# The last pair's second layer as three passes over 12-bit words, in a state-space and ELU layer kernel on one core

## Chip, cores and metric

The kernel runs on one core of a Trainium2 chip. The metric is device time in microseconds (us) of one execution, as the median of several runs. TensorE (PE) multiplies, VectorE (DVE), ScalarE (ACT) and GpSimd (POOL) work element by element, SyncE (SP) issues most transfers. All data that the engines touch lies in SBUF, products arrive in PSUM (eight banks; GpSimd can't reach them).

## What is computed

A chunked state-space scan (4 batches, 8 heads, 768 steps, head width 32, state 16) gives x, a matrix of 3072 tokens by 256. Two dense layers with an ELU between them follow. Cut to the part that matters here:

```python
def _moe_ref(x, w_in, w_out):          # x 3072x256, w_in 256x2048, w_out 2048x256
    h = x @ w_in
    g = np.where(h > 0.0, h, np.exp(np.minimum(h, 0.0)) - 1.0)
    return (g @ w_out).astype(np.float32)
```

All of it is float32.

## The kernel before

**Blocks, pairs and stages.** Tokens are taken in 12 blocks of 256 (`NP` = 12) and, from block 2 on, in pairs (2, 3), (4, 5) up to (10, 11). The inner dimension of 2048 is cut into `MC` = 16 slices m of 128. Every engine runs its instructions in the order in which the code issues them; tiles come from pools in which a tag has a fixed number of buffers that go round, so that a new tile waits for the last use of the tile whose buffer it takes. The loop `for n in range(4, NP, 2)` (L1310) is a row of stages. In the stage of n the pair (n, n+1) goes through the first layer, one slice m = k per step (`l1_words`, L778), while the generator `second(n - 2)` (L871) puts the second layer of the pair before between these products, three or four steps at a time (`l2s`). The stage of n = 10 is the last: it has no scan work left (`m` is None). Behind the loop the second layer of the last pair, `second(10, True)`, runs alone (L1355).

**First layer in words.** An f32 product takes TensorE several passes. The first layer instead cuts both operands into a high word and a rest of about 12 bits, held as f32 tiles of type F32R, which one pass multiplies. Scaled words are used so that three passes give the product: `high` collects w1·y1 and w0·y0, `both` collects the product of the two mixed words, and `WORD - 1` and `WORD` (2 to the 12th) bring the scales together (L788 to L800). ELU follows: L805 and L806 on ScalarE, L813 on VectorE, which writes `g_of[n, m]`, a tile of 128 x 2 blocks x 256 tokens. `end_words` runs one step late (`late`).

**Second layer by sums.** `second` uses seven products in the place of eight (a Strassen-Winograd scheme) on quarters of g and of `w_out`, in plain f32. Sums of activations are made by GpSimd through `sub` (L848): one for every even slice in `end_words` (L816), `sum_t2` (L863), and the eight per half behind products 0 and 1 (L920 to L927). They are made in place, in `g_of`. Of the weights, `a_out` holds four quarters of `w_out`, of which `a_out[2]` (named s1 or a21) was overwritten in place by its sum with `a_out[3]` (`plus`, L1280), and `s_out` holds three more sums, in tiles of tag "w64". Each half of the inner dimension runs seven products r of four steps, whose results VectorE adds into `c`. In the last call (`last`) the second half stores its parts as they are done, with one product split into two (L888 to L900).

**Pools that the change uses.** "w64" (11 buffers: raw weights, then weight sums and the words of w_in), "w_in" (9: the weights and then their third words w0), "g0" and "g1" (12 each: g_of), "L", "bct", "ctm", "xr", "bc", "M", "ec", "b" (scan tiles, out of use in the last stage), "yT" (2), "t2" (4). Of PSUM `p_a` has 7 banks and `p_o` one.

Of the kernel before, what the change touches and what calls it, by code (L numbers as in the profile page):

```python
# [10 lines left out]
F32 = mybir.dt.float32  # L11
U32 = mybir.dt.uint32
BF16 = mybir.dt.bfloat16
F32R = mybir.dt.float32r
ALU = mybir.AluOpType
ACT = mybir.ActivationFunctionType

P = 128
Q = 64
BLK = 2 * P  # L20
CW = 256
WORD = 2.0 ** 12
NEAR = 1.0 + 2.0 ** -13
# [9 lines left out]
def kernel(  # L33
# [27 lines left out]
    nc = tc.nc  # L61
# [3 lines left out]
    NP = NB * NG  # L65
    BH = NB * NH
    ROWS = BH * NG
    DM, DF = moe_w_in.shape
    w_in64, w_out64 = moe_w_in.bitcast(U32), moe_w_out.bitcast(U32)
    KC, MC = DM // P, DF // P  # L70
# [12 lines left out]
    def psum(shape, name):  # L83
        return p_a.tile(shape, F32, tag="a", name=name)
# [7 lines left out]
    for k in range(4):  # L92
        (nc.scalar if k % 2 else nc.sync).dma_start(
            out=la0[BH * k:BH * (k + 1)],
# [715 lines left out]
    def end_words():  # L810
        n, m, h, e = late.pop(0)
        g_of[n, m] = ffn.tile([P, 2, BLK], F32, tag=f"g{m % 2}", name="g", bufs=12)
        nc.vector.scalar_tensor_tensor(  # L813
            out=g_of[n, m].rearrange("p b i -> p (b i)"), in0=e, scalar=1.0, in1=h,
            op0=ALU.subtract, op1=ALU.max)
        if m % 2 == 0 and (n, m) != (2, 14):  # L816
            sub(g_of[n, m][:, 1], g_of[n, m][:, 1], g_of[n, m][:, 0])

    def row_of(n):
        b, g = place(n)  # L820
        return b * S + g * BLK
# [25 lines left out]
    def sub(out, in0, in1):  # L847
        nc.gpsimd.tensor_tensor(out=out, in0=in0, in1=in1, op=ALU.subtract)  # L848

    def quarters(n, i):  # L850


        if n == 2 and i < DIRECT:
            A, B = g_of[n, i], g_of[n + 1, i]
            return A[:, 0], A[:, 1], B[:, 0], B[:, 1]
        A, B = g_of[n, 2 * i], g_of[n, 2 * i + 1]
        return A[:, 0], B[:, 0], A[:, 1], B[:, 1]
# [10 lines left out]

    c_of = {}

    def second(n, last=False):  # L871


        c = c_of[n] = ffn.tile([P, 2, 2, 2, P], F32, tag="c", name="c_sum", bufs=1)
        c11, c12, c21, c22 = (c[:, at, :, e] for e in range(2) for at in range(2))
        a11, a12, s1, a22 = a_out
        s2, s3, s4 = s_out
        for half in range(2):
            if not half:
                tmp = ffn.tile([P, 3, 2, P], F32, tag="tmp", name="p_sum", bufs=1)  # L880
                p1, p5, u = (tmp[:, r] for r in range(3))
            chunk = range(4 * half, 4 * half + 4)

            def add(out, in0, in1, eng=nc.vector):
                eng.tensor_tensor(out=out, in0=in0, in1=in1, op=ALU.add)

            for r, a in enumerate((a11, a12, s1, s2, s3, a22, s4)):
                if last and half and r == 6:  # L888
                    store(n, 0)
                    for ts, queue in enumerate((nc.scalar, nc.sync)):  # L890
                        ps = psum([P, P], "ps_o")
                        for i in chunk:
                            nc.tensor.matmul(  # L893
                                out=ps, lhsT=quarters(n, i)[3][:, ts * P:(ts + 1) * P],
                                rhs=a[:, i], start=(i == chunk[0]), stop=(i == chunk[-1]))
                        nc.vector.tensor_tensor(
                            out=c12[:, ts], in0=ps, in1=c12[:, ts], op=ALU.add)
                        r0 = row_of(n + 1) + ts * P
                        queue.dma_start(out=out[r0:r0 + P, 0:P], in_=c12[:, ts])
                    return  # L900
                pool, tag = (p_a, "a") if (7 * half + r) % 2 else (p_o, "o")
                ps = pool.tile([P, 2, P], F32, tag=tag, name="ps_o")
                for i in chunk:
                    b11, b21, b12, b22 = quarters(n, i)
                    b = (b11, b21, b12, t2_of[n, i], b11, b21, b22)[r]
                    for ts in range(2):
                        nc.tensor.matmul(  # L907
                            out=ps[:, ts], lhsT=b[:, ts * P:(ts + 1) * P], rhs=a[:, i],
                            start=(i == chunk[0] and ts == 0), stop=(i == chunk[-1]),
                            skip_group_check=True)  # L910
                    if i < chunk[-1]:
                        yield
                if r == 0:
                    if half:
                        add(p5, ps, c22)
                        add(c21, ps, c21)
                        add(c11, ps, c11)
                    else:
                        nc.scalar.copy(out=p1, in_=ps)
                    for i in chunk:  # L920
                        b11 = quarters(n, i)[0]
                        sub(b11, t2_of[n, i], b11)
                elif r == 1:
                    add(c11, ps, c11 if half else p1)
                    for i in chunk:
                        b21 = quarters(n, i)[1]
                        sub(b21, b21, t2_of[n, i])  # L927
                elif r == 2:
                    add(p5, ps, p5 if half else p1)
                elif r == 3:  # L930
                    add(p5, ps, p5)
                    if half:
                        add(c12, c12, p5, nc.gpsimd)
                        add(c21, ps, c21)
                    else:
                        add(u, ps, p1)
                elif r == 4:
                    if half:
                        add(c21, ps, c21)
                    else:  # L940
                        add(u, ps, u)
                    add(c22, ps, p5)
                    if not half:
                        nc.scalar.copy(out=c12, in_=ps)  # L944
                    if last and half:
                        r0 = row_of(n + 1)
                        nc.sync.dma_start(
                            out=out[r0:r0 + BLK, P:2 * P].rearrange("(t p) c -> p t c", p=P),
                            in_=c22)
                    if not half:  # L950
                        sum_t2(n, 1)
                    elif n + 2 < NP:
                        sum_t2(n + 2, 0)
                elif r == 5:
                    add(c21, ps, c21 if half else u)
                elif half:
                    add(c12, ps, c12)
                else:
                    nc.vector.tensor_tensor(out=c12, in0=ps, in1=c12, op=ALU.subtract)
                yield  # L960

    def store(n, at):
        r0 = row_of(n + at)
        nc.sync.dma_start(
            out=out[r0:r0 + BLK, :].rearrange("(t p) e -> p t e", p=P),
            in_=c_of[n][:, at].rearrange("p t e c -> p t (e c)"))
# [343 lines left out]
    for n in range(4, NP, 2):  # L1310
        m = n + 2 if n + 2 < NP else None
        steps = second(n - 2)

        def l2s(count):
            for _ in range(count):
                next(steps)

        for k in range(16):
            l1_words(n, k, between=m if k == 15 else None)
            turn_step(n, k // 2 * 2 + 1, k % 2)  # L1320
            if n == 4 and k == 0:
                decay(6, 1)
            if m:
                stage_scan(n, k)
            begin_end()
            if k == 0 and n > 4:
                store(n - 4, 0)
                store(n - 4, 1)
            if not m:
                l2s(4 if k % 2 else 3)  # L1330
                continue
            l2s((3 + (n == 4), 3 - (n == 4), 3, 3, 3, 3, 3, 3, 4 + 4 * (n == 4), 5 - 4 * (n == 4),
                 2, 2, 3, 1, 1, 0)[k])
            if k == 9:
                scores(m, m + 1)
                sums(m, m + 1)
                for q in range(4):
                    weigh_two(m, q)
                l2s(2)
                states(m)  # L1340
            if k == 10:
                states(m + 1)
            if k == 13:
                y = across(m, m + 1)
                inside(y, m, m + 1, ts=(0,))
                l2s(4)
                inside(y, m, m + 1, ts=(1,))
        if m:
            l2s(4)
            both_of_y(m)  # L1350
        end_words()
        for _ in steps:
            pass
    n = NP - 2
    for k, _ in enumerate(second(n, True)):  # L1355
        if k == 0:
            store(n - 2, 0)
            store(n - 2, 1)


# [28 lines left out]
```

## Time and profile before

| what | value |
|---|---|
| runs before | 347.66, 347.88, 347.88 us, median 347.88 |
| the profiled execution, its own time | 347.65 us |
| its span in the profile | 345.9 us |
| granted TensorE clock over the span | 0.999 |
| TensorE idle in all, by its busy time | 345.9 - 338.7 = 7.2 us |
| longest wait of TensorE | 1.1 us (the first product) |
| L799 and L813, VectorE, 72 each | 0.69 us each, one operand in PSUM |
| L848, GpSimd, 128x256 | 0.73 us each (the "g<-t,g" group: 721 to 740 ns) |

The page of the profile gives busy time by engine, the span in 40 slices, the chain of work that ended last, and groups of instructions by line. PE is the matmul side of TensorE, PEld its weight loads, which overlap it. A timeline line is: start, duration, engine, line, operation, output<-inputs, shapes, count; where a count is over 1 the duration is that of the whole run. An f32 product shows as two records. A group is one line of the code with one set of operands; where a helper such as `sub` issues everything, its line stands for many places, and the tile names tell them apart.

### The profile page before, as it was taken

The numbers are of one execution on the slowest core, as the hardware profiler recorded it, in microseconds if no ns is written. First come the engines' busy times: TensorE is split into PE (matmuls) and PEld (weight loads), VectorE is DVE, ScalarE is ACT, GpSimd is POOL, SyncE is SP. The second block draws the span as 40 slices with busy tenths as digits, with TensorE's granted clock in tenths as the row PEclk, the third lists the DMA queues.
The fourth block names the chain that finished last, engine by engine and source line by source line (L and its number), as shares of the span: only waits on it lengthen the run. The fifth ranks groups of instructions, "written<-read, shape, count | busy, mean of one in ns | idle before, by whom it ended". The sixth has DMA issues, their size and how long they took to land.

```text
span 345.9 us, 9861 instructions
## 1 busy us (share of the span) xinstructions
PE 338.7 (98%) x3878; PEld 297.4 (86%) x3878; DVE 253.3 (73%) x504; ACT 238.1 (69%) x541; POOL 215.3 (62%) x321
## 2 busy tenths in 40 slices
PE   8989999999999999999999999999999999999996
PEld 4669888888788898889899888999988999999996
DVE  4898988879898778866788676878676766665222
ACT  5688989599759898657699457699457566565000
POOL 5553553559989699964396664296754264455760
PEclk9999999999999999999999999999999999999999
DMA  8888988470797961070511170410000100001001
GB/s 145 228 231 165 326 178 236 87 140 30 107 151 112 139 108 31 10 162 2 124 45 32 17 153 5 116 22 3 2 0 4 63 0 3 0 0 63 2 1 62
DMA packets 76902, 28.58 MB, mean 83 GB/s; under 512 B 57848, under 2 KB 71736, under 8 KB 76856
## 3 DMA queue, kind: packets, MB, share of 16 engines
q1 hardware_dynamic: 70360, 25.60, 32.2%
q0 software_dynamic: 4176, 2.10, 5.4%
q8 instruction: 30, 0.49, 0.6%
q10 hardware_dynamic: 2320, 0.26, 0.5%
q14 instruction: 16, 0.13, 0.1%
HBM read 22.51 MB, written 3.34 MB: 75 GB/s over the span
## 4 chain that ended last, share of the span: by engine, by line
PE 92%; SPq 2%; DMA 2%; DVE 1%; ACT 1%; issue 1%; POOL 0%; POOLq 0%; ACTq 0%
PE ps_o L907 36%; PE ps_h L788 19%; PE ps_h L671 11%; PE ps_w L788 10%; PE ps_o L832 8%; PE ps_y L638 3%; DMA w<-in_moe_w_in_dram 2%; PE ps_g L545 2%; PE ps_y L620 2%; PE ps_st L575 1%; SPq L179 1%; PE ps_o L893 1%; SPq L132 0%; POOL w_in L252 0%; SPq L116 0%
## 5 line engine op out<-in xcount | busy, mean ns | idle before, releaser
L907 PEld LDWEIGHTS ps_o<-w_out,g 128*128 128x128 f32 x640 | 78.6, 192 | 3.4
L907 PE MATMUL ps_o<-w_out,g 128*128 128x128 f32 x640 | 80.3, 276 | 0.0
L805 ACT ACTIVATE e<-ps_h 128x512 f32<-128x512 f32 x72 | 43.0, 597 | 50.2 <-DVE ps_h L799 50.1
L813 DVE SCALAR_TENSOR_TENSOR g<-e,ps_h 128x512 f32<-128x512 f32 x72 | 49.4, 686 | 34.1 <-ACT e L806 33.7
L848 POOL TENSOR_TENSOR g<-g 128x256 f32<-128x256 f32 x36 | 28.0, 777 | 56.2 <-DVE g L813 56.0
L799 DVE SCALAR_TENSOR_TENSOR ps_h<-ps_h,e 128x512 f32<-128x512 f32 x72 | 50.1, 695 | 12.5 <-ACT e L796 9.7
L788 PE MATMUL ps_w<-y_both,w_words 128*128 128x512 f32 x144 | 51.1, 435 | 0.0
L796 ACT ACTIVATE e<-ps_w 128x512 f32<-128x512 f32 x72 | 42.2, 587 | 12.9 <-PE ps_w L788 12.8
L671 PE MATMUL ps_h<-yT,w_in 128*128 128x256 f32 (+1 forms) x208 | 45.2, 368 | 2.3 <-POOL w_in L252 2.2
L806 ACT ACTIVATE e<-e 128x512 f32<-128x512 f32 x72 | 45.5, 632 | 2.3
L788 PE MATMUL ps_h<-y,w_words 128*128 128x512 f32 x144 | 46.1, 402 | 0.0
L788 PE MATMUL ps_h<-y,w 128*128 128x512 f32 x144 | 44.7, 392 | 0.0
L671 PEld LDWEIGHTS ps_h<-yT,w_in 128*128 128x128 f32 x208 | 36.4, 190 | 8.3 <-POOL w_in L252 3.7
L525 ACT ACTIVATE L<-L,ncum 128x64 f32<-128x64 f32 x160 | 42.2, 336 | 0.2
L907 PE MATMUL ps_o<-w_sum,g 128*128 128x128 f32 x304 | 38.4, 275 | 0.0
L907 PEld LDWEIGHTS ps_o<-w_sum,g 128*128 128x128 f32 x304 | 37.0, 192 | 1.2 <-ACT c_sum L944 0.2
L530 POOL TENSOR_SCALAR_AFFINE_SELECT L<-L 64x512 f32<-64x512 f32 x40 | 30.0, 749 | 9.1 <-ACT L L525 7.7
L788 PEld LDWEIGHTS ps_h<-y,w 128*128 128x128 f32 x144 | 27.1, 188 | 6.5 <-POOL w L848 0.2
L848 POOL TENSOR_TENSOR g<-t,g 128x256 f32<-128x256 f32 x40 | 28.0, 730 | 5.9 <-PE ps_o L907 5.7
L788 PEld LDWEIGHTS ps_h<-y,w_words 128*128 128x128 f32 x144 | 26.4, 188 | 5.7 <-issue 0.4
L832 PE MATMUL ps_o<-w_out,g 128*128 128x256 f32 x128 | 31.0, 384 | 0.0
L848 POOL TENSOR_TENSOR t<-g 128x256 f32<-128x256 f32 x40 | 28.6, 746 | 0.2
(131 smaller groups left out, 535.1 us busy)
## 6 DMA issues: line engine op xcount, KB each, us to landing
L<-flat SPq DMA_DIRECT2D x20, 256.0 KB
w<-in_moe_w_out_dram SPq DMA_DIRECT2D x8, 512.0 KB
w<-in_moe_w_in_dram SPq DMA_DIRECT2D x7, 512.0 KB
xr<-in_x_dram SPq DMA_DIRECT2D x24, 128.0 KB
out_dram<-c_sum SPq DMA_DIRECT2D x9, 256.0 KB
bc<-in_B_dram SPq DMA_DIRECT2D x24, 64.0 KB
w_sum<-w_out POOLq DMA_DIRECT2D x3, 512.0 KB, 8.9
bc<-in_C_dram SPq DMA_DIRECT2D x22, 64.0 KB
```

What stands on the lines that cost most here:

```text
L525: nc.scalar.activation(L[:, h, u], L[:, h, u], ACT.Exp, bias=ncum[:, u, row:row + 1])
L530: nc.gpsimd.affine_select(out=part, in_=part, pattern=[[0, 4], [0, 2], [1, Q]], compare_op=ALU.is_ge, fill=0.0, base=0, channel_multiplier=-1)
L671: nc.tensor.matmul(out=ps[:, j, toks], lhsT=w_in[i][:, k, j * P:(j + 1) * P], rhs=yT[n // 2][:, k, n % 2].rearrange("p u i -> p (u i)")[:, ...
L788: nc.tensor.matmul(out=ps, lhsT=lhs[:, k], rhs=rhs[:, k], start=k == 0 and lhs is not w0, stop=k == KC - 1 and lhs is not w1)
L796: nc.scalar.activation(e, both, ACT.Copy, scale=WORD)
L799: nc.vector.scalar_tensor_tensor(out=high, in0=high, scalar=WORD - 1.0, in1=e, op0=ALU.mult, op1=ALU.add)
L805: nc.scalar.activation(e, high, ACT.Relu, scale=-1.0)
L806: nc.scalar.activation(e, e, ACT.Exp, scale=-1.0)
L813: nc.vector.scalar_tensor_tensor(out=g_of[n, m].rearrange("p b i -> p (b i)"), in0=e, scalar=1.0, in1=h, op0=ALU.subtract, op1=ALU.max)
L832: nc.tensor.matmul(out=o_of[n][:, ts], lhsT=g_of[n, j][:, m % 2, ts * P:(ts + 1) * P], rhs=w_out[:, m], start=(m == 0 and ts == 0), stop=( ...
L848: nc.gpsimd.tensor_tensor(out=out, in0=in0, in1=in1, op=ALU.subtract)
L907: nc.tensor.matmul(out=ps[:, ts], lhsT=b[:, ts * P:(ts + 1) * P], rhs=a[:, i], start=(i == chunk[0] and ts == 0), stop=(i == chunk[-1]), s ...
```

## The change

The pair (10, 11) no longer uses `second`. Its second layer becomes `second_words`, three passes over words, as in the first layer: 16 slices x 4 token tiles t x 3 kinds of word, each a 128x128 word of g against a 128x256 word of `w_out`, into four PSUM banks (one per t; kind 1 in the upper half of the bank, kinds 0 and 2 in the lower).

- **Words of w_out**, by pieces p of two slices: `high_of_out` (ScalarE), `rest_of_out` (VectorE one word, GpSimd through `sub` the other). Pieces 0 to 4 are made in the last stage, 5 to 7 inside `second_words`.
- **Words of g**, by slice: `high_of_g` (ScalarE), `rest_of_g` (VectorE, two words of 128x512). Slices 0 and 1 and the high words of 2 and 3 are made in the last stage, with the rest of slice 2 at its last step; the other words inside `second_words`, four slices ahead on ScalarE and three on VectorE. The loop reaches m + 3 = 15 at m = 12, and `rest_of_g(n, MC - 1)` stands once more behind the loop.
- **Order of the products:** slice by slice for m = 0 to 13; then for each t the three kinds over m = 14 and 15, and at once that tile's copy (ScalarE), sum (VectorE) and store of 128 KB (SP).
- **`given_back`** takes the sum out of `a_out[2]` again (GpSimd, two halves, at k = 4 and 12), since the words need the plain weights.
- **Left out:** for the last pair the sums in `end_words` and `sum_t2`, and the `last` branch of `second`. The last `end_words` of the last stage moves from behind the stage to slice 1 of `second_words`.
- Words lie in buffers of the scan's tags, of "w64", "w_in", "g0", "g1" and "yT". From slice 5 on a new word's buffer in "w_in" is that of a word four or five slices back, so VectorE's second word of slice m waits until the products of slice m - 4 or m - 5 are done.

```diff
-        if m % 2 == 0 and (n, m) != (2, 14):
+        if m % 2 == 0 and (n, m) != (2, 14) and n + 2 < NP:
             sub(g_of[n, m][:, 1], g_of[n, m][:, 1], g_of[n, m][:, 0])
...
-                    elif n + 2 < NP:
+                    elif n + 4 < NP:
                         sum_t2(n + 2, 0)
...
+    def given_back(rows):
+        sub(a_out[2][:, rows], a_out[2][:, rows], a_out[3][:, rows])
...
+    def high_of_out(p):
...
+        for part, rows in parts_of(v[0], p):
+            nc.scalar.activation(part, w_out[:, rows], ACT.Copy, scale=NEAR)
...
+    def rest_of_out(p):
+        v1 = v_of[p][0]
+        for part, rows in parts_of(v_of[p][1], p):
+            high = v1[0] if len(v1) == 1 else v1[rows.start % 2]
+            nc.vector.scalar_tensor_tensor(
+                out=part, in0=high.bitcast(F32), scalar=1.0 / WORD - 1.0, in1=w_out[:, rows],
+                op0=ALU.mult, op1=ALU.add)
+        for part, rows in parts_of(v_of[p][2], p):
...
+            sub(part, w_out[:, rows], high.bitcast(F32))
...
+    def high_of_g(n, m):
...
+        nc.scalar.activation(tiles[0], g_of[n, m], ACT.Copy, scale=NEAR / WORD)
+    def rest_of_g(n, m, which=(1, 2)):
+        for k in which:
+            nc.vector.scalar_tensor_tensor(
+                out=h_of[m][k], in0=h_of[m][0].bitcast(F32), scalar=(1.0 - WORD, WORD)[k - 1],
+                in1=g_of[n, m], op0=ALU.mult, op1=(ALU.add, ALU.subtract)[k - 1])
+    def second_words(n):
+        ps = [psum([P, 2, DM], "ps_o") for _ in range(4)]
+        def product(m, t, kind):
+            lhs = h_of[m][kind][:, t // 2, t % 2 * P:(t % 2 + 1) * P]
+            nc.tensor.matmul(
+                out=ps[t][:, int(kind == 1)], lhsT=lhs, rhs=out_words(m // 2, kind, m),
+                start=(m == 0 and kind == 1), stop=(m == MC - 1 and kind > 0),
+                skip_group_check=True)
+        store(n - 2, 0)
+        store(n - 2, 1)
+        for m in range(MC - 2):
+            if m + 4 < MC:
+                high_of_g(n, m + 4)
+            if m + 3 < MC:
+                rest_of_g(n, m + 3)
+            if m == 1:
+                end_words()
+            if m in (0, 2, 4):
+                high_of_out(5 + m // 2)
+            if m in (1, 3, 5):
+                rest_of_out(5 + m // 2)
+            for t in range(4):
+                for kind in (1, 0, 2):
+                    product(m, t, kind)
+        rest_of_g(n, MC - 1)
+        for t in range(4):
+            for kind in (1, 0, 2):
+                for m in (MC - 2, MC - 1):
+                    product(m, t, kind)
+            o = ffn.tile([P, DM], F32, tag="t2", name="o", bufs=4)
+            nc.scalar.activation(o, ps[t][:, 1], ACT.Copy, scale=WORD)
+            nc.vector.scalar_tensor_tensor(
+                out=o, in0=ps[t][:, 0], scalar=WORD - 1.0, in1=o, op0=ALU.mult, op1=ALU.add)
+            r0 = row_of(n + t // 2) + t % 2 * P
+            nc.sync.dma_start(out=out[r0:r0 + P, :], in_=o)
...
                 l2s(4 if k % 2 else 3)
+                if k in (4, 12):
+                    given_back(slice(k // 2 - 2, k // 2 + 2))
+                if k in (5, 6, 7, 8, 13):
+                    high_of_out(min(k - 5, 4))
+                if k in (6, 7, 8, 9, 14):
+                    rest_of_out(min(k - 6, 4))
+                if k in (2, 10, 14):
+                    high_of_g(n, (2, 10, 14).index(k))
+                if k in (3, 11):
+                    rest_of_g(n, k // 8, (1,))
+                if k in (4, 12):
+                    rest_of_g(n, k // 8, (2,))
+                if k == 15:
+                    rest_of_g(n, 2)
+                if k == 15:
+                    high_of_g(n, 3)
                 continue
...
-        end_words()
+        if m:
+            end_words()
         for _ in steps:
             pass
-    n = NP - 2
-    for k, _ in enumerate(second(n, True)):
-        if k == 0:
-            store(n - 2, 0)
-            store(n - 2, 1)
+    second_words(NP - 2)
```

In the changed kernel the lines are: `high_of_out` L981, `rest_of_out` L996 (its `sub` L848), `high_of_g` L1021, `rest_of_g` L1026, the products L1036, a tile's copy L1063, sum L1064 and store L1067.

More of the change, by code (lines that the diff above doesn't have):

```diff
@@ L869, with second @@
     c_of = {}
-    def second(n, last=False):
+    def second(n):
         c = c_of[n] = ffn.tile([P, 2, 2, 2, P], F32, tag="c", name="c_sum", bufs=1)
@@ L887, in second @@
             for r, a in enumerate((a11, a12, s1, s2, s3, a22, s4)):
[L888 to L900, printed above, removed]
                 pool, tag = (p_a, "a") if (7 * half + r) % 2 else (p_o, "o")
@@ L944, in second @@
                         nc.scalar.copy(out=c12, in_=ps)
[L945 to L949, printed above, removed]
                     if not half:
                         sum_t2(n, 1)
-                    elif n + 2 < NP:
+                    elif n + 4 < NP:
                         sum_t2(n + 2, 0)
@@ L960, in second, with rooms @@
                 yield
+    v_of, h_of = {}, {}
+    def given_back(rows):
+        sub(a_out[2][:, rows], a_out[2][:, rows], a_out[3][:, rows])
+    def rooms(tag, count):
+        pool, bufs, shape = {
+            "bct": (att, 2, [P, 2, DM]), "ctm": (att, 2, [P, 2, DM]), "xr": (raw, 3, [P, 2, DM]),
+            "bc": (raw, 2, [P, 2, DM]), "M": (att, 8, [P, DM]), "ec": (att, 4, [P, DM]),
+            "b": (raw, 2, [P, DM]), "yT": (ffn, 2, [P, 2, 2, DM])}[tag]
+        tiles = [pool.tile(shape, F32R, tag=tag, name="v", bufs=bufs) for _ in range(count)]
+        if len(shape) == 2:
+            return [t.unsqueeze(1) for t in tiles]
+        return [t[:, k] for t in tiles for k in range(2)] if len(shape) == 4 else tiles
@@ new lines @@
+    HOMES = [(("bct", 2), ("ctm", 1)), (("ctm", 1), ("xr", 2)), (("xr", 1), ("bc", 2)), (("M", 6),),
+             (("M", 2), ("ec", 4)), None, (("yT", 1),), (("yT", 1), ("b", 2))]
+    def high_of_out(p):
+        if p == 5:
+            tiles = [conv.tile([P, 2, 2, DM], F32R, tag="w64", name="v", bufs=W_AHEAD) for _ in range(2)]
+            spare.append(tiles[1][:, 1])
+            tiles = [tiles[0][:, 0], tiles[0][:, 1], tiles[1][:, 0]]
+        else:
+            tiles = [t for tag, count in HOMES[p] for t in rooms(tag, count)]
+            if p == 6:
+                tiles.append(spare.pop())
+        per = len(tiles) // 3 if len(tiles) != 4 else None
+        v = [[], [], []]
+        if per is None:
+            v = [[tiles[0]], [tiles[1]], tiles[2:]]
+        else:
+            v = [tiles[k * per:(k + 1) * per] for k in range(3)]
+        v_of[p] = v
+        for part, rows in parts_of(v[0], p):
+            nc.scalar.activation(part, w_out[:, rows], ACT.Copy, scale=NEAR)
@@ new lines, in parts_of, with out_words @@
+    def parts_of(tiles, p):
+        count = 2 // len(tiles)
+        return [(t, slice(2 * p + at * count, 2 * p + (at + 1) * count)) for at, t in enumerate(tiles)]
+    def out_words(p, kind, m):
+        tiles = v_of[p][kind]
+        return tiles[0][:, m % 2] if len(tiles) == 1 else tiles[m % 2][:, 0]
+    def rest_of_out(p):
[6 more added lines that the diff above has]
+        for part, rows in parts_of(v_of[p][2], p):
+            high = v1[rows.start % 2 if len(v1) == 2 else 0]
+            if len(v1) == 1 and len(v_of[p][2]) == 2:
+                high = high[:, rows.start % 2:rows.start % 2 + 1]
+            sub(part, w_out[:, rows], high.bitcast(F32))
@@ new lines @@
+    spare = []
+    def high_of_g(n, m):
+        if m == 0:
+            both = att.tile([P, 2, 2, BLK], F32R, tag="L", name="g_words", bufs=2)
+        elif m == 1:
+            both = att.tile([P, 2, 2, BLK], F32R, tag="L", name="g_words", bufs=2)
+        if m < 2:
+            tiles = [both[:, 0], both[:, 1], conv.tile(
+                [P, 2, BLK], F32R, tag="w_in", name="g_words", bufs=DF // CW + 1)]
+        else:
+            tiles = [conv.tile([P, 2, BLK], F32R, tag="w_in", name="g_words", bufs=DF // CW + 1)
+                     for _ in range(2)]
+            tiles.append(ffn.tile([P, 2, BLK], F32R, tag=f"g{m % 2}", name="g_words", bufs=12))
+        h_of[m] = tiles
+        nc.scalar.activation(tiles[0], g_of[n, m], ACT.Copy, scale=NEAR / WORD)
```

## The prediction

> **What bounds the kernel now.** I read the busy shares of the page first, then a table of three stretches, then the chain of waits at its end, then timelines of single engines where two of them meet.
>
> ```profile
> PE 338.7 (98%) x3878; PEld 297.4 (86%) x3878; DVE 253.3 (73%) x504; ACT 238.1 (69%) x541; POOL 215.3 (62%) x321
> ```
> TensorE is busy over 98% of the span of 345.9 us, so only less TensorE time, or a wait put in its way, can move the end. The stretches are the last stage (first layer of the last pair, with the second layer of the pair before it), the last pair's second layer alone, and the tail; the columns are busy time of each engine, granted clock, DMA share, GB/s.
>
> ```profile
> 267.10:317.40 50.30, 50.30 (x352) 46.37 (x352) 33.02 (x58) 30.33 (x54) 23.80 (x34) 1.00 0.05 17
> 317.40:342.70 25.30, 25.27 (x227) 25.07 (x225) 8.49 (x21) 1.84 (x4) 14.51 (x21) 1.00 0.07 23
> 342.70:346.00 3.30, 0.00 (x0) 0.00 (x0) 0.29 (x1) 0.00 (x0) 0.00 (x0) 0.90 0.24 75
> ```
> The last stage leaves VectorE 17.3 us, ScalarE 20.0 and GpSimd 26.5 of its 50.3 free. The second layer alone uses VectorE 8.5 us of 25.3: that is the space the change fills.
>
> ```profile
> 314.49 0.92 PE ps_h L788 x4
> 315.42 0.45 PE ps_w L788 x2
> 315.87 25.01 PE ps_o L907 x224
> 340.88 1.80 PE ps_o L893 x16
> 342.68 0.02 issue
> 342.70 0.29 DVE c_sum L896
> ```
> The chain of waits is TensorE without a gap up to 342.68. The first 16 of the 224 still belong to the pair before (16 x 0.1116 = 1.79), so the last pair's layer runs from T0 = 317.66 to 342.68: 14 products of 16 records, 224 records in 25.02 us, 0.1117 each. Behind it lie 3.25 us of one sum, a DMA issue and its landing, which in some form every version pays.
>
> **The change part by part.** *TensorE.* The 224 records give way to 16 x 4 x 3 = 192 products of a 128x128 word with a 128x256 word. No row has that shape. A record of L907 is half of an f32 product over 128 columns, with a weight load of its own; at 512 columns L788 takes 0.46 per two (0.23 each, 315.42 to 315.87 above). Bounds: 0.1116 as L907, or 0.115 as half of L788, from below; from above the 0.19 that a weight load lasts in the groups of the page (L907 PEld, mean 192 ns), if loads were not hidden. L907 streams a load with every 0.1116 already and moves the same number of columns through the array, so I take 0.1116: 192 x 0.1116 = 21.4 us, 3.6 us less. Were VectorE never late, TensorE would end at 339.1.
>
> *VectorE makes the words, and this is what I think decides.* For each of the 16 slices m of the activations ScalarE makes a high word (L1021) and VectorE two more (L1026, 128x512, both inputs in SBUF). The nearest row is L773, the same form:
>
> ```profile
> 269.76 0.42 DVE L885 TENSOR_TENSOR c_sum<-ps_o,c_sum 128x256 f32<-128x256 f32 x1
> 270.09 1.29 DVE L773 SCALAR_TENSOR_TENSOR y_both<-y,yT 128x512 fp32r<-128x512 f32 x2
> 271.29 0.69 DVE L813 SCALAR_TENSOR_TENSOR g<-e,ps_h 128x512 f32<-128x512 f32 x1
> ```
> One lasts 0.69 but the next starts 0.60 after it (two from 270.09 to 271.29). Slices 0 and 1 are finished in the last stage. Slice 2's pair stands on VectorE behind the last c12 sum of the pair before, which started at 317.76 and lets go at about 318.10. From there VectorE's queue holds: pairs for m = 2 to 15 (28), the pair for m = 15 a second time (it is called once in the loop, at m = 12, and again behind the loop: 2 more), the last L813, and three L996 for weight pieces 5, 6, 7. That is 34 x 0.60 = 20.4 us, to 338.5. Each pair also waits on semaphores; two L763 with such waits took 1.36 instead of 1.20 (267.20 to 268.56), so 15 pairs cost 0 to 2.4 more; I take half of it, 1.2: 339.7. So on a good day VectorE just keeps up.
>
> *GpSimd gets in its way.* Three weight pieces have their low words made by GpSimd in the same stretch (L848: two of 128x512, two of 128x256). ScalarE reaches piece 5 at about 320.3, piece 6 at 322, piece 7 at 324 (0.62 each, behind the high words of m = 3 to 8), so GpSimd's three fall between 320 and 327, when VectorE does nothing but reads of two SBUF operands. What happens then the trace shows around 77 us:
>
> ```profile
> 76.98 2.37 DVE L763 SCALAR_TENSOR_TENSOR y<-y,yT 128x512 fp32r<-128x512 f32 x2
> 79.27 1.14 DVE L738 SCALAR_TENSOR_TENSOR w_words<-w_words,w_in 128x512 fp32r<-128x512 f32 x1
> ...
> 81.41 2.01 DVE L773 SCALAR_TENSOR_TENSOR y_both<-y,yT 128x512 fp32r<-128x512 f32 x2
> ...
> 77.20 1.59 POOL L252 TENSOR_TENSOR w_out<-mag,w_out 128x512 uint32<-128x512 uint32 x1 [1.49 <-DVE mag L242]
> 78.75 2.18 POOL L530 TENSOR_SCALAR_AFFINE_SELECT L<-L 64x512 f32<-64x512 f32 x2
> 81.02 1.86 POOL L848 TENSOR_TENSOR w<-w_in,w_words 128x256 fp32r<-128x256 f32 x2
> ```
> The two L763 took 2.37 instead of 1.29, the two L773 2.01 instead of 1.29, and GpSimd's were longer too (two of L848 1.86; alone 0.73 each). From 81.02 to 83.42 is 2.40, about the sum of both alone, 1.46 + 1.29 less an overlap: they take turns, an instruction at a time. Where VectorE reads one operand from PSUM (L799, L813) GpSimd is not hurt: its 40 "g<-t,g" range from 721 to 740 ns. GpSimd alone needs 2 x 1.27 (L252, 128x512, shortest) + 2 x 0.73 = 4.0 us; 0.6 of it can lie under the last L813. Bounds 0 (GpSimd always yields) to 4.0; both rows in which they meet have VectorE paying about what the other holds, so 3.4. VectorE's last word: 343.1.
>
> The Trainium skill, "GPSIMD Engine Reference", section Key points, says that GpSimd shares its SBUF interfaces with VectorE and collides with instructions of two SBUF inputs; it gives no price. By it the collision is certain, by the two rows alone likely; the trace agrees (2.01 against 1.29), and it speaks against just this mix of engines.
>
> *What is late next.* Products up to m = 4 have their words in time (T0 + 5 x 1.34 = 324.4). Product 5 waits for m = 5: 318.1 + three pairs + L813 + L996 + one pair at 1.28 and 0.6, plus 3.4, is 327.8; from there TensorE follows VectorE, 1.28 against its own 1.34 a slice, with 0.6 more at pieces 6 and 7. Behind the loop the first output tile needs both words of m = 15, so the second making of them is waited for in full (1.2 to 1.3 us of the sum). Then 19 products are left: 19 x 0.1116 = 2.1, with 0.1 to start: TensorE ends at 345.3 instead of 342.68, +2.6.
>
> *The end.* Each tile now needs a ScalarE copy (128x256, 0.37), then a sum on VectorE (0.42, the L885 row, against 0.29 for L896), then its 128 KB store on SP's queue; the three earlier stores are 0.7 us apart and done with before. The copy can start when the tile's first two products are in, or only after all six: 0 to 0.5. I add 0.13 + 0.17 + 0.1 = 0.4.
>
> *Costed at nothing.* In the last stage ScalarE gets 7 L981 and 4 L1021 (at most 6 us of 20 free), VectorE 4 L1026 and L996 worth 5 of full size (5.4 of 17.3), GpSimd two L848 on w_out and seven on v (9.2 us) while twelve L848 of 0.73 for the Strassen sums go (8.8). The cover is the depth of PSUM: a first-layer bank comes round after 7 allocations, nearly three slices of 3 us (the one that L813 lets go at 286.6 is wanted near 291, 4.4 us later); the single ps_o bank is wanted again after one product and one first-layer slice, some 3 us, less the sum itself about 2.5. One extra VectorE instruction a slice, 0.6, doubled where GpSimd is in the way, fits; if not, the price is 0.5 to 2 us. The two stores that stood in the old tail's SP queue are the same two, as early as before.
>
> **The sum.** +2.6 + 0.4 = +3.0 on the profiled execution: span 345.9 to 348.9, its own time 347.65 to 350.65. The median of the runs stands 0.23 above that execution, so 350.8.
>
> **The rivals.**
> *GpSimd yields (not slower).* One mechanism, at the shared reads from 320 to 327. If GpSimd waits for VectorE and not the reverse, VectorE ends at 338.5 to 339.7 and TensorE at 340.7 to 341.9; with the 0.4 that is -1.6 to -0.4: 346.3 to 347.5. For it: L738 at 110.20 lasted 0.68 next to a GpSimd pair of 2.12. Against it: the two meetings above. It decides as soon as GpSimd costs VectorE less than about 0.4 us (1.6 without semaphore time). Chance 0.24.
> *The last stage stalls too.* A second-layer sum stands behind a word and a GpSimd pass, ps_o comes free late, TensorE waits 0.5 to 2 us there, on top of the forecast: 351.5 to 353. Against it: TensorE has no wait at all there now. 0.15.
> *The clock drops.* TensorE stands still about 3 us before product 5. The granted clock is 1.00 up to the end now, and TensorE's waits are 1.1 us at the longest, so the trace cannot say what 3 us does. Half clock for some 3.4 us would lose 1.7 us of products: 352.5. Chance 0.06. The Trainium skill, "TensorE: Matmul & The Clock Gate", Part 1, has the clock halve after an idle window of about 3.4 us, which the stall only just reaches.
> *The products cost the weight load.* 192 x 0.19 = 36.5 us, 15 more than reckoned: about 358. Against it: L907 streams loads at 0.1116. 0.02.
>
> **How the numbers follow.** The forecast, 349.6 to 352.0 for semaphore time of 0 to 2.4, keeps 0.53. A measurement of this kernel tells 0.2%, 0.7 us, from no change: faster is below 347.2. The first rival gives 0.16 faster and 0.08 the same; of the rest 0.76 is slower. The range 346.5 to 352.9 leaves out a little of the first rival and the dearest cases.
>
> **What would show it.** Right: L1026 pairs above 1.4 us from 320 to 327 and about 1.2 to 1.3 afterwards; TensorE idle before the products ended by L1026; VectorE near fully busy from 318 to 343; the repeated pair of m = 15 on the chain of waits. Wrong: TensorE gapless to 339; L1026 at 0.60 throughout; a gap in the last stage; a granted clock under 1.

## The result and the profile after

The changed kernel takes 350.75 us (median of 6 runs, 349.93 to 351.57) against 347.77 (6 runs, 347.17 to 348.00): a ratio of 1.009, with a 95% interval of 1.0073 to 1.0107, so some 3.0 us slower. The profiled execution took 351.57 us, with a span of 349.8 against 345.9.

Page of the changed kernel, busy time by engine, then the three stretches of before, the last one to the end of the span:

```profile
PE 340.6 (97%) x3846; PEld 297.7 (85%) x3846; DVE 276.9 (79%) x532; ACT 251.5 (72%) x569; POOL 208.7 (60%) x301
```
```profile
267.10:317.40 50.30, 50.30 (x350) 46.23 (x349) 39.23 (x69) 32.86 (x62) 26.36 (x31) 1.00 0.04 12
317.40:342.70 25.30, 22.98 (x174) 22.13 (x173) 24.37 (x37) 11.59 (x21) 5.11 (x4) 0.93 0.07 22
342.70:350.00 7.30, 3.27 (x27) 3.06 (x26) 2.31 (x6) 1.54 (x4) 0.00 (x0) 0.91 0.22 73
```
The last stage still fills TensorE (50.30 of 50.30). In the stretch of the second layer VectorE went from 8.49 to 24.37 us of 25.3, TensorE fell to 22.98, and the granted clock, 1.00 before, to 0.93. The end of the chain of waits:

```profile
316.31 1.78 PE ps_o L894 x16
318.09 5.84 PE ps_o L1036 x47
324.16 1.77 DVE g_words L1026
325.98 1.15 PE ps_o L1036 x8
327.12 1.15 DVE g_words L1026
328.31 17.66 PE ps_o L1036 x132
```
TensorE runs through slices 0 to 3, then waits for VectorE's words at slice 4 (twice) and slice 5, then runs to 345.96. The layer takes 27.87 us in the place of 25.02. Its parts: 192 products at 0.1204 (from the run of products alone, below) 23.1; 1.8 more for the last 132, which took 17.66 where 132 x 0.1204 is 15.9; the rest, 3.0, is the waits (the list of waits, which counts from the modelled end of a product, has 2.3 of it). VectorE and GpSimd in that stretch, from their timelines:

```profile
319.63 1.28 DVE L1026 SCALAR_TENSOR_TENSOR g_words<-g_words,g 128x512 fp32r<-128x512 f32 x2
321.24 4.68 DVE L1026 SCALAR_TENSOR_TENSOR g_words<-g_words,g 128x512 fp32r<-128x512 f32 x4 [0.33 <-ACT g_words L1021]
...
327.04 3.02 DVE L1026 SCALAR_TENSOR_TENSOR g_words<-g_words,g 128x512 fp32r<-128x512 f32 x4
...
333.60 9.71 DVE L1026 SCALAR_TENSOR_TENSOR g_words<-g_words,g 128x512 fp32r<-128x512 f32 x16
```
```profile
322.33 1.36 POOL L848 TENSOR_TENSOR v<-w_out,v 128x512 fp32r<-128x512 f32 x1 [5.97 <-ACT v L981]
323.89 3.83 POOL L848 TENSOR_TENSOR v<-w_out,v 128x512 fp32r<-128x512 f32 x3 [0.20 <-ACT v L981]
```
Undisturbed, 16 words take 9.71 us, 0.607 each. Beside GpSimd's four instructions four words take 4.68 in the place of 2.4, and the next four 3.02. VectorE ends its last word at 343.31; TensorE, slowed by its clock, gets to it some 0.4 us later (19 products before 345.96). Last the clock, in windows of 2 us (columns as above, the clock third from the end):

```profile
324.00:326.00 2.00, 0.56 (x4) 0.32 (x3) 2.00 (x3) 1.37 (x3) 1.92 (x2) 1.00 0.00 0
326.00:328.00 2.00, 1.43 (x10) 1.23 (x10) 2.00 (x3) 0.63 (x1) 1.71 (x2) 1.00 0.00 0
328.00:330.00 2.00, 1.69 (x7) 1.58 (x8) 2.00 (x5) 0.00 (x0) 0.00 (x0) 0.54 0.00 0
330.00:332.00 2.00, 2.00 (x13) 2.00 (x13) 2.00 (x5) 0.63 (x1) 0.00 (x0) 0.61 0.00 0
332.00:334.00 2.00, 2.00 (x19) 2.00 (x18) 2.00 (x4) 0.63 (x1) 0.00 (x0) 1.00 0.00 0
```
Behind the waits TensorE gets half its clock for 3.4 us (in windows of 0.5 us the clock reads 0.50 in each from 328.5 to 331.5). That happened in this execution (mean clock 0.993); the other five have 0.998 to 1.000 and take 349.93 to 351.02, so the drop is not what made the kernel slower.

### The profile page after: what moved, and what is told of

The parts are those of the page before. It is cut to its first block, busy times and chain, and to the rows that moved or that the text cites. A ratio compares the mean times of both kernels' runs of the same rounds, so it can differ in the third digit from the quotient of the medians.

```text
span 349.8 us, 9822 instructions
## 1 busy us (share of the span) xinstructions
PE 340.6 (97%) x3846; PEld 297.7 (85%) x3846; DVE 276.9 (79%) x532; ACT 251.5 (72%) x569; POOL 208.7 (60%) x301
## 4 chain that ended last, share of the span: by engine, by line
PE 91%; SPq 2%; DMA 2%; DVE 2%; ACT 1%; issue 1%; POOL 0%; DVEq 0%; POOLq 0%; ACTq 0%
PE ps_o L894 29%; PE ps_h L788 19%; PE ps_h L671 11%; PE ps_w L788 10%; PE ps_o L832 8%; PE ps_o L1036 7%; PE ps_y L638 3%; DMA w<-in_moe_w_in_dram 2%; PE ps_g L545 2%; PE ps_y L620 2%; PE ps_st L575 1%; DVE g_words L1026 1%; SPq L179 1%; SPq L132 0%; POOL w_in L252 0%
## 5 line engine op out<-in xcount | busy, mean ns | idle before, releaser
L894 PEld LDWEIGHTS ps_o<-w_out,g 128*128 128x128 f32 x512 | 64.0, 191 | 3.4
L894 PE MATMUL ps_o<-w_out,g 128*128 128x128 f32 x512 | 65.3, 275 | 0.0
L799 DVE SCALAR_TENSOR_TENSOR ps_h<-ps_h,e 128x512 f32<-128x512 f32 x72 | 50.0, 694 | 12.5 <-ACT e L796 11.7
L788 PE MATMUL ps_w<-y_both,w_words 128*128 128x512 f32 x144 | 51.2, 435 | 0.0
L788 PE MATMUL ps_h<-y,w_words 128*128 128x512 f32 x144 | 46.1, 402 | 0.0
L788 PE MATMUL ps_h<-y,w 128*128 128x512 f32 x144 | 44.7, 392 | 0.0
L848 POOL TENSOR_TENSOR g<-g 128x256 f32<-128x256 f32 x28 | 22.3, 796 | 35.8 <-DVE g L813 35.5
L788 PEld LDWEIGHTS ps_h<-y,w 128*128 128x128 f32 x144 | 27.0, 188 | 6.6 <-POOL w L848 0.2
L894 PE MATMUL ps_o<-w_sum,g 128*128 128x128 f32 x256 | 32.5, 275 | 0.0
L894 PEld LDWEIGHTS ps_o<-w_sum,g 128*128 128x128 f32 x256 | 31.4, 192 | 1.2 <-ACT c_sum L931 0.2
L788 PEld LDWEIGHTS ps_h<-y,w_words 128*128 128x128 f32 x144 | 26.4, 188 | 5.8 <-issue 0.4
L1036 PE MATMUL ps_o<-v,g_words 128*128 128x256 f32 x192 | 25.8, 296 | 2.3 <-DVE g_words L1026 2.3
L1036 PEld LDWEIGHTS ps_o<-v,g_words 128*128 128x128 f32 x192 | 24.8, 201 | 3.2 <-DVE g_words L1026 2.9
```

The lines of the kernel that those rows point to most:

```text
L788: nc.tensor.matmul(out=ps, lhsT=lhs[:, k], rhs=rhs[:, k], start=k == 0 and lhs is not w0, stop=k == KC - 1 and lhs is not w1)
L799: nc.vector.scalar_tensor_tensor(out=high, in0=high, scalar=WORD - 1.0, in1=e, op0=ALU.mult, op1=ALU.add)
L894: nc.tensor.matmul(out=ps[:, ts], lhsT=b[:, ts * P:(ts + 1) * P], rhs=a[:, i], start=(i == chunk[0] and ts == 0), stop=(i == chunk[-1]), s ...
L1036: nc.tensor.matmul(out=ps[t][:, int(kind == 1)], lhsT=lhs, rhs=out_words(m // 2, kind, m), start=(m == 0 and kind == 1), stop=(m == MC - 1 ...
```

## The experiments

The theory: VectorE bounds the layer, because its words start late, because GpSimd takes turns with it, and because slice 15 is made twice. The rival: TensorE bounds it, by products dearer than reckoned and by its clock. All ratios are to the kernel before on the same chip.

**Slice 15 made once** (e1).

```diff
-        rest_of_g(n, MC - 1)
         for t in range(4):
```


> The words of slice 15 are made once. In the changed kernel VectorE ends its last word at 343.3 us, just when TensorE reaches it; in that profile TensorE was also held back 1.7 us by half a clock, so without that it would have waited. If VectorE bounds the layer: 1.2 us less VectorE work is about 1.0 to 1.2 us less time, 349.5 to 349.8 against 350.75. Rival, TensorE bounds it (products at 0.120 us, clock): the second making was hidden, 350.4 to 350.9.

Measured: 350.28 us, ratio 1.0082 (1.0065 to 1.0099). That lies between the ranges of the two: the gain is 0.5 us by the medians and 0.3 by the ratios, where the theory asked for 1.0 to 1.2, and the intervals of the two kernels overlap. The single executions tell more: four of six had the half clock (0.993 to 0.994) and took 350.21 to 350.97; the two without it took 349.14 and 349.43, about 1.4 below the changed kernel's own without it (median 350.72), of which some 0.4 is the chip (the kernel before: 347.37 here, 347.77 there). So the repeat costs about 1.0 us where the clock holds, by two executions only. Where the clock drops it is hidden: both profiled executions have the drop, and the layer takes 27.76 us here (317.03 to 344.79) and 27.87 in the changed kernel. Nearly all of the 1.2 us between their spans lies ahead of the layer, which starts at 317.03 in the one and 318.09 in the other; from one profile to the next that start moves by up to 1.06 us, so layers are compared from their own start below. Both theories have a share.

**No low words by GpSimd** (e2), **both edits** (e3).

```diff
-        for part, rows in parts_of(v_of[p][2], p):
+        for part, rows in parts_of(v_of[p][2], p) if p < 5 else ():
...
-        tiles = v_of[p][kind]
+        tiles = v_of[p][0 if p > 4 and kind == 2 else kind]
```


> GpSimd makes no low words for weight pieces 5 to 7; the products of these pieces read the high word in their place (same count of products, other numbers). If GpSimd and VectorE take turns at shared reads: the four L1026 that lasted 4.68 us take 2.4, VectorE's last word comes 2.5 to 2.9 us earlier, the first long wait of TensorE goes, and the time falls to 347.8 to 348.4. Rival, TensorE bounds it or GpSimd costs VectorE nothing: 350.0 or more.

> The two edits together: slice 15 made once, and no low words of pieces 5 to 7 by GpSimd (the products read the high word there). VectorE theory: the last word comes about 4.1 us earlier, near 339.2, and TensorE is close to gapless behind 318.1: 347.0 to 347.5. If each edit alone gains nothing, this one does not either.

Measured: 347.82, ratio 1.0017 (1.0006 to 1.0028), and 347.19, ratio 0.9996 (0.9987 to 1.0005), both as the VectorE theory has it. VectorE's timeline of e2:

```profile
318.74 1.28 DVE L1026 SCALAR_TENSOR_TENSOR g_words<-g_words,g 128x512 fp32r<-128x512 f32 x2
320.36 2.50 DVE L1026 SCALAR_TENSOR_TENSOR g_words<-g_words,g 128x512 fp32r<-128x512 f32 x4 [0.33 <-ACT g_words L1021]
...
323.97 2.49 DVE L1026 SCALAR_TENSOR_TENSOR g_words<-g_words,g 128x512 fp32r<-128x512 f32 x4
...
329.99 9.72 DVE L1026 SCALAR_TENSOR_TENSOR g_words<-g_words,g 128x512 fp32r<-128x512 f32 x16
```
The four words of 4.68 take 2.50, those of 3.02 take 2.49, nothing else changes: 2.7 us less from first word to last (23.68 to 20.97), and no execution of e2 or e3 is under a clock of 0.997. Most of the loss was the four GpSimd instructions: 2.5 us of 3.0 by the ratios. With GpSimd out of the way the repeat is on the chain of waits of e2:

```profile
335.50 3.62 DVE g_words L1026 x6
339.16 3.15 PE ps_o L1036 x23
```
It is worth 0.7 us by the ratios (1.0017 to 0.9996), and the layer goes from 25.13 to 24.35 us. With both out of the way the kernel takes as long as before.

**Products alone** (e4): the words of slices 3 to 15 go, so the result is not the layer's.

```diff
-            if m + 4 < MC:
-                high_of_g(n, m + 4)
-            if m + 3 < MC:
-                rest_of_g(n, m + 3)
...
-            lhs = h_of[m][kind][:, t // 2, t % 2 * P:(t % 2 + 1) * P]
+            lhs = h_of[min(m, 2)][kind][:, t // 2, t % 2 * P:(t % 2 + 1) * P]
```


> The words of activation slices 3 to 15 are left out, the products of these slices read slice 2's words; count and form of products are unchanged, slice 15 is not made twice. What is left is TensorE's own pace. With the 0.1204 us a product seen in the profile: 318.1 + 192 x 0.1204 = 341.2, span 345.1, time 346.7 to 347.1, only about 1 us under the kernel before. With the 0.1116 that the prediction took: 339.5, time 345.0 to 345.4. If the time stays near 350, it is neither VectorE nor the words, but the last stage or the tail.

Measured: 345.93, ratio 0.9960 (0.9947 to 0.9974), 1.4 us under the kernel before: the ceiling of the idea as built. The time lies between the two ranges, 0.8 under the one for 0.1204, of which 0.65 is the start of the layer, 317.45 where 318.1 was taken. The price is settled by the chain of waits, in one piece:

```profile
317.45 23.12 PE ps_o L1036 x192
```
23.12 / 192 = 0.1204 a product, not 0.1116. Words that cost nothing would have gained 1.4 us; words without GpSimd and without a repeat (e3) gain nothing clear of the noise, with 1.2 us of waits left in the layer (24.35 against 23.12); as the change makes them they lose 3.0.

**Waits filled** (e5): 18 products into an unused bank where TensorE waits, on top of e1.

```diff
...
+            if m == 5:
+                fill(8)
             for t in range(4):
                 for kind in (1, 0, 2):
+                    if (m, t, kind) == (4, 0, 2):
+                        fill(10)
                     product(m, t, kind)
```


> Base is the run without the repeat (350.28). Where TensorE waits for words of slices 4 and 5, 18 products into an unused bank are put in (10 inside slice 4, 8 before slice 5, 0.120 us each = 2.2 us, about as long as it waits); their result is not read. If the half clock after these waits (3.4 us, 1.7 us of products lost) comes from TensorE's idleness, the granted clock stays at 1.00, and the time is that of the base's own executions without the drop: 349.1 to 349.5. Rival, the drop has another cause or costs nothing: 350.2 or, where the fill is on the path, up to 351.

Measured: 350.01 (349.66 to 350.13), ratio 1.0074 (1.0060 to 1.0087), clock 0.997 to 1.000 in all six. The clock held, as it should if idleness is the cause. But that the filling did it is not shown: e7 below, with the same waits left open and on the same chip, held its clock in five of six executions, and the four drops of e1 came on another chip. The time missed, 0.5 above the range. In its profile the layer takes 27.2 us from its first product in the timeline to its last, just as in e7's profile, whose clock held too; with the drop it is 28.0 in e1's. So the filling costs nothing that shows, and the drop costs e1 some 0.8 us. The range rested on two executions of e1; why e5 stands above them stays open. Of its layer the last 130 products took 16.18 us, 0.1245 each, 0.5 us more than at 0.1204; whether that is short waits for words was not tried.

**Copies early** (e7, on e1), **low words by VectorE** (e8, on e1).

```diff
...
+        for t in range(4):
+            for m in (MC - 2, MC - 1):
+                product(m, t, 1)
+            os.append(ffn.tile([P, DM], F32, tag="t2", name="o", bufs=4))
+            nc.scalar.activation(os[t], ps[t][:, 1], ACT.Copy, scale=WORD)
...
```
```diff
-            sub(part, w_out[:, rows], high.bitcast(F32))
+            (nc.vector if p > 4 else nc.gpsimd).tensor_tensor(
+                out=part, in0=w_out[:, rows], in1=high.bitcast(F32), op=ALU.subtract)
```


> Base is the run without the repeat (ratio 1.0082). In the last two slices the kind-1 products of all four tiles come first and each tile's ScalarE copy behind them; kinds 0 and 2 follow. The copy and its wait, about 0.38 to 0.45 us between the last product and the last sum, leave the end: 0.3 to 0.5 us less, ratio about 1.007. If the copy was hidden already: no change; if TensorE now waits for the copies (same bank), up to 0.5 more.

> Base is the run without the repeat. The low words of pieces 5 to 7 are made by VectorE in place of GpSimd: three more instructions of 0.6 on the engine that is thought to bound. If turns at the shared reads cost VectorE 2.9 us, it still ends 1.1 us earlier, the long waits of TensorE shrink, and the clock stays up: 348.0 to 348.7. If GpSimd's part cost VectorE nothing, 1.8 us more: about 351.5.

Measured for e7: 349.72, ratio 1.0070 (1.0052 to 1.0088), as expected by its number and not by its reason. Only one of its six executions had the half clock (351.03; the others 349.13 to 349.87), against four of e1's on another chip, and in its profile TensorE ends at 344.27 with 3.83 us behind it, against 3.81 in e1: the copies have left the chain, but now the four sums and stores come at once, and SP issues them 0.53 us apart. The end is not shorter. Measured for e8: 349.24, ratio 1.0054 (1.0035 to 1.0074): 1.0 us under e1, although the engine that bounds makes the low words of three pieces too; less was gained than expected, 0.5 above the range. VectorE takes 21.63 us from its first word to its last, against 22.49 in e1, and TensorE's waits for words shrink from 2.3 to 1.1 us in the list of waits.

**A piece in plain f32** (e6, on e8 with e7's order). Slices 12 and 13 make no words; their f32 products run behind slice 4.

```diff
+        words = list(range(12)) + [14, 15]
+        whole_g = ffn.tile([P, 2, 2, BLK], F32, tag="yT", name="g_scaled")
...
+            if at < 2:
+                nc.scalar.activation(whole_g[:, at], g_of[n, 12 + at], ACT.Copy, scale=1.0 / WORD)
...
+            if at == 4:
+                for k in range(2):
+                    for t in range(4):
+                        nc.tensor.matmul(
+                            out=ps[t][:, 1], lhsT=whole_g[:, k, t // 2, t % 2 * P:(t % 2 + 1) * P],
+                            rhs=w_out[:, 12 + k], start=False, stop=False, skip_group_check=True)
```


> A version meant to beat both: slice 15 made once; low words of pieces 5 and 7 by VectorE; slices 12 and 13 (piece 6) as plain f32 products of g/4096 into the upper half of the banks, put behind slice 4 where TensorE waited; the kind-1 products of the last two slices first, so that the copies of all tiles lie beside products. VectorE has 29 instructions of 0.6 from about 1.9 us behind the layer's start, 19.3 us in; TensorE needs slice 15 at 318.1 + 12 x 1.445 + 3.6 = 339.0, 20.9 in: VectorE in time. TensorE 14 x 1.445 + 3.6 = 23.8 us against 25.0 before, tail 3.45 to 3.85 against 3.25: 0.4 to 1.0 us under the kernel before (ratio 0.997 to 0.999). If VectorE still bounds: 0.5 us or more over it.

Measured: 346.58, ratio 0.9980 (0.9968 to 0.9993), as expected: 0.6 us under the kernel before here, and so faster than both. In the chain of waits the layer has no VectorE word in it:

```profile
317.90 7.31 PE ps_o L1037 x60
325.21 3.46 PE ps_o L1065 x16
328.67 11.54 PE ps_o L1037 x96
```
Two variants of it. **Two queues** (e9): stores of tiles 1 and 3 on ScalarE's queue. **Plain piece late** (e10): the plain products behind slice 11.

```diff
-            nc.sync.dma_start(out=out[r0:r0 + P, :], in_=o)
+            (nc.sync, nc.scalar)[t % 2].dma_start(out=out[r0:r0 + P, :], in_=o)
```
```diff
-            if at == 4:
+            if at == 11:
                 for k in range(2):
```


> Base is e6_plain_piece (ratio 0.998), where the last four sums run 0.48 us apart and SP's queue takes 0.53 us an issue, so that the last issue ends 0.72 us behind the last sum, against 0.36 in the changed kernel. Two of the four stores go to ScalarE's queue: the last issue follows the last sum at once, 0.3 to 0.4 us less, ratio about 0.997. If SP's issue was not what held the end back: no change.

> Base is e6_plain_piece. The eight plain products stand behind slice 11 in place of slice 4; all work is the same. If they help as cover for VectorE's late words, TensorE now waits 0.7 to 1.2 us at slices 4 to 6 again: ratio 1.000 to 1.002. If only VectorE's smaller load mattered, no change from 0.998.

Measured: e9 346.58, ratio 0.9983 (0.9973 to 0.9992), no change, a miss: from the layer's first product in the timeline to the end of the span it is 27.8 us in e6 and 27.9 in e9. The last issue does end sooner, 0.40 us behind the last sum in the place of 0.72, but from there to the end it is 2.9 us in the place of 2.6, so the issue on SP was not what held the end. e10 348.71, ratio 1.0034 (1.0022 to 1.0047): the same work in another order costs 1.9 us, more than expected. From first product to last the layer takes 25.7 us against 24.0 in e6. TensorE waits at slices 5 and 9:

```profile
325.70 6.62 PE L1037 MATMUL ps_o<-v,g_words 128*128 128x256 f32 x50 [0.70 <-DVE g_words L1027]
332.48 4.31 PE L1037 MATMUL ps_o<-v,g_words 128*128 128x256 f32 x34 [0.16 <-DVE g_words L1027]
```
These two make 0.9 us; the products behind them, 84 in 10.93 us where 84 x 0.1204 is 10.1, hold the other 0.8, which the list of waits does not break down. So the plain products gain as cover for the words, not by sparing VectorE work alone.

## The prediction against the runs, point by point

- **Direction and size** held: 350.8 said, 350.75 measured, with slower at 0.76. That it came within 0.05 us is luck, since several terms were off and made up for one another. TensorE's layer was to be 21.4 us of products and 6.2 of waits; in the profile it was 23.1 of products, 3.0 of waits and 1.8 of half clock. VectorE's last word, 343.1 said, came at 343.31: 1.5 of later start, less 0.7 of turns and 0.6 of semaphore time.
- **The bound** held: VectorE, near fully busy from 318 to 343, and TensorE idle before products, ended by L1026. Of the signs of being right the repeated pair on the chain of waits is missing in the profiled execution (it is there in e2); of the signs of being wrong a lower clock came, 0.993 in that execution alone.
- **GpSimd's turns**: 3.4 us said, 2.7 measured (the four and four words against e2); the rival in which GpSimd yields is refuted. The waits came at slice 4 and slice 5, the longest 1.2 us, and not as one stand of 3 us before product 5.
- **The product's price** was mis-sized: "I take 0.1116" from L907; e4 shows 0.1204, 1.7 us more over 192. L788, the same kind of operand, was the better row: its half, 0.115, would have left 1.0 of the 1.7. What the half misses is a part that does not shrink with the columns: 0.91 to 0.93 for four of 512 columns is 0.2275 to 0.2325 each, against 0.1204 at 256, which makes 0.107 to 0.112 per 256 columns and a fixed 0.008 to 0.013. Two shapes give such a line without testing it.
- **Semaphore time** of the pairs, 1.2 us said, was about 0.6: one idle time of 0.33 before slice 3's words, and 0.2 as 34 instructions go at 0.607 (16 words in 9.71) and not 0.60.
- **"Costed at nothing", the last stage**: TensorE had no wait there, as said. But the work was not free: it surfaced as a late start of VectorE, 319.63 where 318.10 was said, 0.4 of it because the whole layer stands 0.43 later in this execution, so 1.1 is its own. Of this chain the kernel before shows, for slice 15:

```profile
315.90 0.60 ACT L796 ACTIVATE e<-ps_w 128x512 f32<-128x512 f32 x1 [0.65 <-PE ps_w L788]
316.54 0.70 DVE L799 SCALAR_TENSOR_TENSOR ps_h<-ps_h,e 128x512 f32<-128x512 f32 x1 [0.56 <-ACT e L796]
```
and the changed one:

```profile
310.92 1.11 DVE L1026 SCALAR_TENSOR_TENSOR g_words<-g_words,g 128x512 fp32r<-128x512 f32 x1
311.44 1.75 POOL L848 TENSOR_TENSOR w_out<-w_out 128x512 f32<-128x512 f32 x1
...
314.43 0.71 ACT L981 ACTIVATE v<-w_out 128x256 fp32r<-128x256 f32 x2
...
317.56 0.61 ACT L1021 ACTIVATE g_words<-g 128x512 fp32r<-128x512 f32 x1
318.08 0.58 ACT L796 ACTIVATE e<-ps_w 128x512 f32<-128x512 f32 x1
318.69 0.70 DVE L799 SCALAR_TENSOR_TENSOR ps_h<-ps_h,e 128x512 f32<-128x512 f32 x1 [0.32 <-ACT e L796]
```
A word of 1.11 beside `given_back`, two L981 and one L1021 stand ahead of the ELU chain, whose L799 comes 2.15 us later; the last c12 sum and slice 2's words stand behind it. This is read from the traces; which of these costs most was not tried.
- **The repeat** "is waited for in full": so in e2 (0.7), and where the clock holds (about 1.0 us, by two executions of e1), but hidden in the profiled execution with the half clock.
- **The tail** was said to grow by 0.4; it grew by 0.6, 3.25 to 3.84: a tile's copy waits for all six of its products (the first starts at 343.85, with 18 products or 2.2 us to go before 345.96), the upper end of the bound.
- **The clock's drop**, at 0.06, came in one execution of six, in four of six of e1 and one of six of e7. Its price was too high: the execution with the drop is 0.85 us above the median of the others, and in e1 the layer is 0.8 longer than in e7's profile without it, not 1.7, since TensorE would have waited for words.
- **Two prices of rivals** don't add up as written: 350.8 and 0.5 to 2 is 351.3 to 352.8, and "about 358" is the span (317.66 + 36.5 + 3.65 = 357.8) and not the time. Neither moves the forecast.

## What to carry to other kernels

Take the price of a product from a row with the same operand type, and not from a row with the same pace of loads; where only another width is on record, leave room for a part that doesn't shrink with the columns. When work is moved to idle engines, ask which of them read SBUF at the same time: four GpSimd instructions on the path of a VectorE chain of two-operand reads cost 2.5 us of the 3.0 that the change lost. And where one engine starts late but is faster per step, put work that doesn't need it in the gap: the same eight products were worth 1.9 us at slice 4 over slice 11.

## What was not expected of the hardware

The clock halved with no long idle stretch. Between 324 and 328 us TensorE was busy for 1.99 of 4 us, in three waits of which the longest is 1.2 us in the list of waits, and then it had half its clock for 3.4 us (the windows of 0.54 and 0.61 make 1.8 and 1.6). The Trainium skill, "TensorE: Matmul & The Clock Gate", Part 1, puts half clock behind an idle window of about 3.4 us. No window of that length was idle here: being half busy was enough, in some executions and not in others. That the waits are the cause is likely, since the drop stands right behind them in both profiles that have it, but it is not shown: filled with products of no use they left the clock at 0.997 or more in six of six (e5), and left open on the same chip in five of six (e7).
